# Output product 4 by a second level of Strassen, spread over four slots

## The chip, the cores and the metric

The kernel runs on one core of one Trainium2 chip. The metric is the device time of one launch in microseconds (us), the median of several runs. A profile of one launch stands beside it: start, duration and names of every instruction on the five engines, which are the matrix engine (PE in the profile; its weight loads are PEld), the vector engine (DVE), the scalar engine (ACT), GpSimd (POOL) and SyncE (SP), which here only issues transfers.

## What is computed

The reference is a linear attention, followed by two dense layers with a leaky ReLU between them, all in float32:

```python
kv  = einsum('bhsd,bhse->bhde', k, v)          # 8 batches, 8 heads, 576 rows, 64 wide
out = einsum('bhsd,bhde->bhse', q, kv)
x   = out / sqrt(mean(out*out, -1) + 1e-6) * g_norm   # then (4608, 512)
h   = x @ w_in                                 # 512 -> 2048
y   = maximum(0.01*h, h) @ w_out               # 2048 -> 512
```

## The kernel before

The 4608 rows are cut into nine blocks of 512. Block 0 is multiplied plainly. For blocks 1 to 8 each of the two layers is done in four chunks of the hidden width (`NC` = 4), and each chunk of a layer is one Strassen multiplication in Winograd's form: seven products in place of eight, numbered 1 to 7, whose factors (the "sides") are blocks of the matrices or sums of such blocks. Chunk `n` counts through all blocks: block `i` has n = 4(i-1) to 4(i-1)+3, so blocks 3 to 8 begin at n = 8. I write c for n modulo 4.

In blocks 2 to 8 the first layer has a second level: each of the seven products is itself done as seven products of quarter size (`product_h_two`). One *slot* is one outer product of the first layer: seven matmuls of 128 x 128 x 128, in two PSUM banks (`h_ha` and `h_hb`, in the next slot `h_hc` and `h_hd`, and so on in turn), followed by whatever is placed beside it. A chunk has seven slots, called t = 0 to 6 here, with the outer products in the order 1, 2, 6, 5, 7, 3, 4.

The second layer (`product_o`) runs late: the products of chunk n begin at t = 2 of chunk n+1 and end at t = 1 of chunk n+2, one in each slot after the slot's part of the first layer. Its order in blocks 2 to 8 is `(1, 5, 6, None, 7, 3, 4)`; at `None` the slot has no product of the second layer. Products 1, 6, 7 and 4 are summed one after another in one PSUM bank (`o_a` in even chunks, `o_c` in odd ones), products 5 and 3 in the other; after each product the vector engine adds the bank to one of four output tiles in SBUF (the scalar engine copies it where c = 0 and the tile is new). So product 4 finds 1+6+7 in its bank and the tile of rows 2, columns 1 ("21") takes the whole sum. A bank is written again only after it has been read.

Product 2 of the second layer is already done by a second level (class `Second`): its seven quarter products are matmuls of 128 columns into the free fourth column group of the banks `h_hb` and `h_hd`, one in each slot of chunk n+2, read by the vector engine (`o<-h_hb`, `o<-h_hd`, 128 x 128). Its sums of activation quarters, `gi`, are made on GpSimd by `inner_g`, at t = 4 and 6 of chunk n+1; the sums of weight quarters are made once by `inner_w2`.

Within a slot the instructions of the vector engine stand in program order (they are pinned): first the reads of the slot's first-layer banks, then pieces of the next batch's attention and the sums of the next block's x (around the start of chunk c = 3 these are four sums of 128 x 512 more, two of them at t = 0 and 1), then the read of the second layer's bank. The fresh banks of the first layer are copied by the scalar engine; its order is the scheduler's. At the end of a chunk, after product 4 of the first layer, seven additions on the vector engine (`g<-...`) form the hidden activations and four leaky ReLUs on the scalar engine follow, before the scalar engine's second copy of the next chunk's first slot.

The weight sides of the second layer that are sums (products 5, 6 in `t12`; 7, 4 in `t34`) are kept in DRAM and loaded by SyncE for each chunk: `t12` after product 6, `t34` after product 4 of the chunk before.

Of the kernel before, what the change touches and what calls it, by code (L numbers as in the profile page):

```python
# [23 lines left out]
def kernel(  # L24
# [74 lines left out]
    NW = U * NE * P  # L99
    w1_all = consts.tile([P, 2 * NC * NW], F32, name="w1_all")  # L100
    stage = consts.tile([P, 3 * NW], F32, name="stage")
    pairs = consts.tile([P, 4 * NW], F32, name="pairs")
    g_all = [consts.tile([P, 4 * U * N2], F32, name=f"g_{i}") for i in range(2)]

    def view(t, lo, *shape):
        n = 1
        for d in shape:
            n *= d
        t = t[:, lo:lo + n]
        names = "abcd"[:len(shape)]  # L110
        return t.rearrange(f"p ({' '.join(names)}) -> p {' '.join(names)}",
                           **dict(zip(names, shape))) if len(shape) > 1 else t

    def pair(i, *shape):
        return view(pairs, i * NW, *shape)

    def matmul(*args, **kw):
        pin(nc.tensor.matmul(*args, **kw))  # L118
# [66 lines left out]
    zeros = view(g_all[0], 0, NT)  # L185
    nc.vector.memset(zeros[:, :64], 0.0)
    nc.vector.memset(zeros[:, 64:], 0.0)
    ident = consts.tile([P, P], F32, name="ident")

    def make_ident():  # L190
        pin(nc.gpsimd.memset(ident, 1.0))
# [449 lines left out]
    def sides_w1(c):  # L641
# [9 lines left out]
        def more():  # L651
# [5 lines left out]

    w2_dram = [[dram.tile([P, 2, U, N2], F32, name=f"w2_{c}_{i}") for i in range(2)]
               for c in range(NC)]
    t12, t34 = pair(2, 2, U, N2), pair(3, 2, U, N2)  # L660
    writes = []

    def sides_w2(n):

        c = n % NC
        b11, b12 = w2_sb[0][c][:, :, :N2], w2_sb[0][c][:, :, N2:]
        b21, b22 = w2_sb[1][c][:, :, :N2], w2_sb[1][c][:, :, N2:]

        def sums(i):
            t = (t12, t34)[i]
            if n >= NC:
                pin(nc.sync.dma_start(t, w2_dram[c][i]))
                return
            if i == 0:
                add(nc.gpsimd, t[:, 0], b12, b11, True)
                add(nc.gpsimd, t[:, 1], b22, t[:, 0], True)
            else:
                add(nc.gpsimd, t[:, 0], b22, b12, True)  # L680
                add(nc.gpsimd, t[:, 1], b21, t12[:, 1], True)
            if (n, i) == (NC - 1, 1):

                writes.append((w2_dram[c][i], t))
            else:
                pin(nc.sync.dma_start(w2_dram[c][i], t))
        return {1: b11, 2: b21, 3: b22, 5: t12[:, 0], 6: t12[:, 1], 7: t34[:, 0],
                4: t34[:, 1]}, sums
# [49 lines left out]
    def read(to):  # L738
        nonlocal n_read
        while n_read < min(to, len(reads)):  # L740
# [5 lines left out]
    qc = pair(0, 4, 3, P)  # L746
    xt1 = [work.tile([P, 2, N2], F32, tag="xt1", name="xt1"),
           view(w1_all, RING * NG + 24 * P, 2, N2)]
    xt24 = [work.tile([P, 2, 2, N2], F32, tag="xt24", name="xt24"),
            view(w1_all, RING * NG + 16 * P, 2, 2, N2)]  # L750
    xi = view(stage, 0, 3, 7, P)

    def sides_x(i):


        x = xTs.pop(i)
        b11, b12 = x[:, :2, :N2], x[:, :2, N2:]
        b21, b22 = x[:, 2:, :N2], x[:, 2:, N2:]
        home = i % 2 if i > 1 else 0
        t1, t2, t4 = xt1[home], xt24[home][:, 0], xt24[home][:, 1]  # L760
        if i == 1:
            t4 = opool.tile([P, 2, N2], F32, tag="o", name="xt4", bufs=6)
        t3 = b12
        sides = {1: b11, 2: b21, 3: b22, 4: t4, 5: t1, 6: t2, 7: t3}

        def sums():
            for t, a, b in ((t1, b12, b11), (t2, b22, t1), (t3, b22, b12), (t4, b21, t2)):
                add(nc.vector, t, a, b, True)
                yield

        batches, quarters, at = [], {k: {} for k in ORDER}, 0
        upper, lower = (x[:, h:h + 2, :].rearrange("p r (t v n) -> p t r v n", t=2, v=2)
                        for h in (0, 2))
        for js, y in (((1, 7), upper), ((2, 3), lower),
                      ((6, 4), xt24[home].rearrange("p t r (v n) -> p t r v n", v=2)),
                      ((5,), t1.rearrange("p r (v n) -> p r v n", v=2).unsqueeze(1))):
            terms = [y[:, :, r, v, :] for r in range(2) for v in range(2)]
            terms += [xi[:, k, at:at + len(js), :] for k in range(3)]
            batches.append(terms)
            for n, j in enumerate(js):  # L780
                for k, term in zip((1, 7, 2, 3, 5, 6, 4), terms):
                    quarters[k][j] = term[:, n, :]
            at += len(js)

        def inner(kind):
            for y11, y12, y21, y22, t1, t2, t4 in batches:
                if kind == 0:
                    add(nc.gpsimd, t1, y12, y11, True)
                    add(nc.gpsimd, t2, y22, t1, True)
                elif kind == 1:  # L790
                    add(nc.gpsimd, y12, y22, y12, True)
                else:
                    add(nc.gpsimd, t4, y21, t2, True)

        return sides, quarters, sums(), inner
# [83 lines left out]

    gi = view(pairs, 12 * P, 4, P)

    def inner_w2(c):
        y = w2_sb[1][c]
# [7 lines left out]

    def inner_g(c, half):

        g = g_of(c)[3]
        a11, a21, a12, a22 = (g[:, n, :] for n in range(4))
        s1, s2, s3, s4 = (gi[:, n, :] for n in range(4))
        if half == 0:
            add(nc.gpsimd, s1, a21, a22)  # L900
            add(nc.gpsimd, s2, s1, a11, True)
        else:
            add(nc.gpsimd, s3, a11, a21, True)
            add(nc.gpsimd, s4, a12, s2, True)

    class Second:
# [17 lines left out]
        def done(self, k, bank):  # L924
            v, s = INTO[k]
            to = self.o[:, v, s * P:s * P + P]
            add(nc.vector, to, bank, to)
            if self.n % NC == NC - 1 and k == ORDER[-1]:
                self.finish("11", self.o)

    def product_h_two(i, c, quarters, to, second):

# [41 lines left out]
    def product_o(n, g_sides, os, finish, second):  # L974

        c = n % NC
        w_sides, _ = sides_w2(n)
        sums = sides_w2(n + 1)[1] if n + 1 < NC * (NB - 1) else lambda i: None
        if c == 0:

            for key in ("12", "22", "11", "21"):
                os[key] = opool.tile([P, 2, N2], F32, tag="o", name=f"o{key}", bufs=6)


        pieces = ((0, slice(0, N2)), (1, slice(0, P)), (1, slice(P, N2))) \
            if n + 1 == NC * (NB - 1) else None
        into = {1: ("11", True), 5: ("22", True), 2: ("11", False), 6: ("12", True),
                3: ("12", False), 7: ("22", False), 4: ("21", True)}

        def done(i, bank):  # L990
            key, fresh = into[i]
            if isinstance(bank, list):
                for at, (end, (part, cols)) in enumerate(zip(bank, pieces)):
                    to = os[key][:, part, cols]
                    add(nc.vector, to, end, to)
                    if i == ORDER[-1]:
                        finish(key, os[key], part, cols, (nc.sync, nc.scalar)[at % 2])
                if i == 7:
                    finish(key, os[key])
                return  # L1000
            to = os[key].rearrange("p u (v n) -> p (u v) n", v=2)
            if c == 0 and fresh:
                nc.scalar.copy(to, bank)
            else:
                add(nc.vector, to, bank, to)
            if c == NC - 1 and i in (2, 7, 3, 4):
                finish(key, os[key])

            if i == (6 if second else 5):
                sums(0)  # L1010
            elif i == 4:
                sums(1)


        yield from strassen((("oa", "oc"), ("oc", "oa"))[n % 2], lambda i, part, r: g_sides[i][:, 2 * r + part, :],
                            lambda i, part, r: w_sides[i][:, r, :], done,
                           (1, 5, 6, None, 7, 3, 4) if second else ORDER,
                           pieces=pieces)

    def go(steps, n=None):  # L1020
        while n is None or n > 0:
# [16 lines left out]
    def first_block(between):  # L1038
# [26 lines left out]
                       start=(now[2] == 0), stop=(n == 2 * NC * U))  # L1065
            between(n, 1)
        for t in range(4):
            o = opool.tile([P, DM], F32, tag="o", name="o", bufs=6)
            if t % 2:
                nc.scalar.copy(o, accs[t])  # L1070
            else:
                nc.vector.tensor_copy(o, accs[t])
            nc.scalar.dma_start(out[t * P:(t + 1) * P, :], o)
# [45 lines left out]
    HELD = (22, 24, 26)  # L1119
    o_queue, waited = collections.deque(), 0  # L1120

    seconds = {}

    def second_of(n):
        if n in seconds:
# [9 lines left out]
    for i in range(1, NB):  # L1135
# [4 lines left out]
        for c in range(NC):  # L1140
# [3 lines left out]
            for t in range(7):  # L1144
# [22 lines left out]
                if now - 1 in seconds:  # L1167
                    for half in range(2):
                        if t == (6 if half else 4):
                            inner_g((now - 1) % NC, half)  # L1170
                    if t == 5 and now <= 2 * NC:
                        inner_w2((now - 1) % NC)
                if slot == 4 and not one:
                    while writes:
                        pin(nc.sync.dma_start(*writes.pop()))
# [78 lines left out]
```

## Time and profile before

| | before |
|---|---|
| time, median of 3 | 918.09 us (917.85 to 918.37) |
| span of the profiled launch | 916.1 us, TensorE clock granted 1.000 |
| PE busy | 909.3 us, 99% |
| weight loads | 776.3 us, 85% |
| DVE busy | 631.6 us, 69% |
| ACT busy | 328.2 us, 36% |
| POOL busy | 370.2 us, 40% |
| DMA | 200.05 MB, mean 218 GB/s |

The page gives the busy time of each engine, the span in 40 slices, the chain of work that ended last, and the costliest groups of instructions; single stretches are read from the timeline, one line for each run of like instructions (start, duration, engine, names, shapes, and in brackets the idle time before it with what ended it). A float32 matmul of the program stands in the trace as two records, so a product of four matmuls shows as x8. Durations of PE records overlap; what a matmul takes is read from the distance between starts. The blocks of the second-level part begin, by the first bank `h_ha` of each, at 228.4 (block 2), 326.9, 423.8, 520.7, 617.6, 712.1 and 803.9 us (block 8); the next batch's attention has no more pieces in block 8, and few in block 7.

### The profile page before, as it was taken

To read this page: it belongs to the slowest core of one execution; us is meant where nothing else is said; L and a number is where in the kernel's file an instruction comes from. 1 tells how busy PE (TensorE), PEld (TensorE's weight loads), DVE (VectorE), ACT (ScalarE), POOL (GpSimd) and SP (SyncE) were. 2 spreads that over 40 slices of the span, in tenths; PEclk is the share of its full clock that TensorE was granted. 3 is DMA by queue.
4 is the path that set the end of the run, shared out by engine and by line. 5 is a ranking of instruction groups with operands and counts; after the bars stand their busy time and mean duration, and the time that the engine had idled before them with its cause. 6 is when DMAs were issued, how large, how long until landed. Compare 5 with 4: busy or idle time off the path is not lost.

```text
span 916.1 us, 18037 instructions
## 1 busy us (share of the span) xinstructions
PE 909.3 (99%) x6980; PEld 776.3 (85%) x6980; DVE 631.6 (69%) x1168; ACT 328.2 (36%) x645; POOL 370.2 (40%) x438
## 2 busy tenths in 40 slices
PE   9999999999999999999999999999999999999998
PEld 5444448888998999899999999999999999999997
DVE  4876995587457876587756786678659755755565
ACT  5454533242135233533343324332343333223330
POOL 2000355967633473226421642264226422642222
DMA  8999926885599778776886789658765676667632
GB/s 269 236 245 249 248 85 191 280 285 167 166 360 289 228 209 268 233 230 214 255 247 230 219 249 272 222 178 212 242 183 176 187 222 198 185 185 223 197 109 92
DMA packets 90228, 200.05 MB, mean 218 GB/s; under 512 B 9888, under 2 KB 42272, under 8 KB 90144
## 3 DMA queue, kind: packets, MB, share of 16 engines
q1 hardware_dynamic: 79680, 187.04, 68.6%
q10 hardware_dynamic: 10016, 10.69, 3.4%
q8 instruction: 55, 0.90, 0.4%
q0 software_dynamic: 448, 1.18, 0.3%
q14 instruction: 29, 0.24, 0.1%
HBM read 172.39 MB, written 26.48 MB: 217 GB/s over the span
## 4 chain that ended last, share of the span: by engine, by line
PE 96%; DMA 2%; DVE 1%; issue 0%; ACT 0%; POOL 0%; SPq 0%; ACTq 0%; DVEq 0%; POOLq 0%
PE o_a L118 19%; PE o_c L118 18%; PE h_ha L118 11%; PE h_hb L118 11%; PE h_hc L118 8%; PE h_hd L118 8%; PE o_acc L118 6%; PE h_ps L118 6%; PE o_ps L118 3%; PE h_a L118 2%; PE h_b L118 1%; PE h_c L118 1%; PE h_d L118 1%; PE kv_ps L118 1%; DMA pairs<-in_v_dram 1%; DMA v_in<-in_v_dram 1%
## 5 line engine op out<-in xcount | busy, mean ns | idle before, releaser
L637 POOL TENSOR_TENSOR gs<-g 128x512 f32<-128x512 f32 x64 | 81.7, 1277 | 253.3 <-ACT g L833 253.3
L833 ACT ACTIVATE g<-g 128x512 f32<-128x512 f32 x124 | 78.2, 631 | 131.9 <-DVE g L637 131.9
L952 ACT COPY w_all<-h_ha 128x512 f32<-128x512 f32 x84 | 48.9, 582 | 173.5 <-PE h_ha L118 167.8
L118 PE MATMUL o_a<-pairs,gs 128*128 128x256 f32 x384 | 91.3, 381 | 0.0
L118 PE MATMUL o_c<-pairs,gs 128*128 128x256 f32 x376 | 89.2, 380 | 0.0
L637 DVE TENSOR_TENSOR o<-h_hb,o 128x128 f32<-128x128 f32 x104 | 29.8, 287 | 83.8 <-ACT pairs L952 83.7
L637 DVE TENSOR_TENSOR o<-o_c,o 128x512 f32<-128x512 f32 (+1 forms) x91 | 61.2, 672 | 23.9 <-PE o_c L118 23.6
L118 PEld LDWEIGHTS o_a<-pairs,gs 128*128 128x128 f32 x384 | 69.8, 190 | 9.2 <-POOL pairs L637 1.2
L118 PEld LDWEIGHTS o_c<-pairs,gs 128*128 128x128 f32 x376 | 68.3, 190 | 7.6
L637 DVE TENSOR_TENSOR o<-o_a,o 128x512 f32<-128x512 f32 x75 | 51.2, 683 | 28.2 <-PE o_a L118 28.1
L637 POOL TENSOR_TENSOR pairs<-w_all 128x512 f32<-128x512 f32 x8 | 11.1, 1384 | 120.6 <-ACT cut L245 102.3
L118 PE MATMUL h_ha<-stage,w_all 128*128 128x128 f32 x448 | 59.6, 276 | 0.0
L118 PEld LDWEIGHTS h_ha<-stage,w_all 128*128 128x128 f32 x448 | 56.6, 192 | 3.0 <-issue 0.7
L118 PE MATMUL h_ps<-xT,w_all 128*128 128x512 f32 (+1 forms) x136 | 58.0, 570 | 0.9 <-DVE w_all L258 0.9
L118 PE MATMUL o_acc<-w,g 128*128 128x512 f32 x128 | 57.8, 595 | 0.0
L637 DVE TENSOR_TENSOR g<-g,pairs 128x512 f32<-128x512 f32 x84 | 55.7, 689 | 1.9
L637 POOL TENSOR_TENSOR pairs<-g 128x128 f32<-128x128 f32 x52 | 23.9, 459 | 75.4 <-PE h_hb L118 46.7
L118 PEld LDWEIGHTS h_ps<-xT,w_all 128*128 128x128 f32 x136 | 25.5, 190 | 30.0 <-issue 26.6
L637 DVE TENSOR_TENSOR w_all<-h_hc,w_all 128x512 f32<-128x512 f32 x56 | 38.3, 684 | 15.9 <-PE h_hc L118 15.8
L118 PEld LDWEIGHTS o_acc<-w,g 128*128 128x128 f32 x128 | 24.0, 190 | 29.8 <-issue 29.4
L637 DVE TENSOR_TENSOR o<-h_hd,o 128x128 f32<-128x128 f32 x78 | 22.1, 283 | 37.8 <-ACT pairs L952 37.7
L118 PE MATMUL h_hb<-stage,w_all 128*128 128x128 f32 x336 | 46.7, 275 | 0.0
(228 smaller groups left out, 2264.6 us busy)
## 6 DMA issues: line engine op xcount, KB each, us to landing
w_all<-w SPq DMA_DIRECT2D x196, 448.0 KB, 4.2
pairs<-w SPq DMA_DIRECT2D x56, 512.0 KB, 4.3
out_dram<-o ACTq DMA_DIRECT2D x35, 256.0 KB, 4.6
v_in<-in_v_dram SPq DMA_DIRECT2D x29, 288.0 KB, 5.7
k_in<-in_k_dram SPq DMA_DIRECT2D x28, 288.0 KB, 5.1
q_in<-in_q_dram SPq DMA_DIRECT2D x56, 144.0 KB, 6.0
q_in<-in_q_dram SPq DMA_DIRECT2D x56, 140.0 KB, 5.8
w<-stage SPq DMA_DIRECT2D x12, 512.0 KB, 4.6
```

The source lines that it names most:

```text
L118: pin(nc.tensor.matmul(*args, **kw))
L637: ins = eng.tensor_tensor(out_, a, b_, op=ALU.subtract if minus else ALU.add)
L833: nc.scalar.activation(t, t if src is None else src, func=AF.Prelu, alpha=SLOPE)
L952: nc.scalar.copy(q[:, at], bank)
```

## The change

For chunks n = 8 to 28 (blocks 3 to 7, and the first chunk of block 8: 21 chunks) product 4 of the second layer is no longer four matmuls of 256 columns but seven of 128 columns, a second level as for product 2. It is for saving matrix work: seven quarter products for eight. The parts:

- `Fourth` does the seven in four steps, `(1, 2, 5), (6, 3), (7,), (4,)`, in a fresh tile of the bank that products 1, 6 and 7 have used, in column groups 0 to 2. Step 0 stands in the slot where product 4 was (t = 1 of chunk n+2); steps 1, 2 and 3 stand at t = 2, 3 and 4, after the next chunk's own product of that slot. Each step's matmuls are followed by the vector engine's adds of 128 x 128 into the tile "21" (copies on the scalar engine for c = 0 and quarters 1, 5, 6, 4).
- The order of the other products becomes `(1, None, 6, 5, 7, 3, None)`: the second step is now the empty one, product 5 moves from t = 3 to t = 5, product 6 stays at t = 4.
- As product 4 no longer finds 1+6+7 in its bank, product 7 is added into a tile of its own ("7"), and for c = 3 (and at n = 28) that tile is added to "22" and to "21" by two more additions of 128 x 512.
- `inner_g` makes the sums of quarters for products 2 and 4 at once (128 x 256 in place of 128 x 128). The weight quarters of product 4 with their sums are made once in block 2 (`inner_w4`), written to DRAM, and loaded (448 KB) in place of the 256 KB of the old side 4.
- Output tiles: "11" has two buffers of its own, the others four; the identity matrix takes the place of a tile that is used later.

```diff
+    def four(n):
+        return 2 * NC <= n < NC * (NB - 1) - 3
...
+    class Fourth:
+        STEPS = (1, 2, 5), (6, 3), (7,), (4,)
+        COLUMN = {1: 0, 6: 0, 7: 0, 4: 0, 2: 1, 5: 2, 3: 2}
...
+        def step(self, at):
+            if at == 0:
+                self.bank = ps_m.tile([P, 4, P], F32, tag=self.tag, name=f"f_{self.tag}")
+            for k in self.STEPS[at]:
+                matmul(self.bank[:, self.COLUMN[k], :], lhsT=self.left[k], rhs=self.right[k],
+                       start=(k == 1), stop=True, skip_group_check=True)
+            for k in self.STEPS[at]:
+                bank = self.bank[:, self.COLUMN[k], :]
+                v, s = INTO[k]
+                to = self.o_of("21")[:, v, s * P:s * P + P]
+                if self.n % NC == 0 and k in (1, 5, 6, 4):
+                    nc.scalar.copy(to, bank)
+                else:
+                    add(nc.vector, to, bank, to)
+            if at == 3:
+                self.last()
...
         def done(i, bank):
             key, fresh = into[i]
+            if fourth and i == 7:
+                key, fresh = "7", True
...
-            if c == NC - 1 and i in (2, 7, 3, 4):
+            if fourth and i == 7:
+                sums(1, 0)
+                if c == NC - 1 or not four(n + 1):
+                    add(nc.vector, os["22"], os["22"], os["7"])
+                if c == NC - 1:
+                    finish("22", os["22"])
+            elif c == NC - 1 and i in (2, 7, 3, 4):
                 finish(key, os[key])
...
+        def last():
+            sums(1, 1)
+            if c == NC - 1 or not four(n + 1):
+                add(nc.vector, os["21"], os["21"], os["7"])
...
+        before = fourths.popleft() if fourths else None
+        order = ORDER
+        if fourth or before:
+            order = (1, None, 6, 5, 7, 3, None if fourth else 4)
+        elif second:
+            order = (1, 5, 6, None, 7, 3, 4)
...
+        for j in range(7):
+            next(steps)
+            if before and j < 3:
+                before.step(j + 1)
+            if fourth and j == 6:
+                now.step(0)
+            yield
...
     def inner_g(c, half):
-        g = g_of(c)[3]
-        a11, a21, a12, a22 = (g[:, n, :] for n in range(4))
-        s1, s2, s3, s4 = (gi[:, n, :] for n in range(4))
+        g = view(g_all[c % 2], 0, 4, 4, P)
+        a11, a21, a12, a22 = (g[:, n, 2:, :] for n in range(4))
+        s1, s2, s3, s4 = (gi_two[:, :, n * P:n * P + P] for n in range(4))
```

## The prediction

> **What bounds the kernel now.** I read the page first: busy times, then the chain that ended last.
>
> ```profile
> PE 909.3 (99%) x6980; PEld 776.3 (85%) x6980; DVE 631.6 (69%) x1168; ACT 328.2 (36%) x645; POOL 370.2 (40%) x438
> ...
> PE 96%; DMA 2%; DVE 1%; issue 0%; ACT 0%; POOL 0%; SPq 0%; ACTq 0%; DVEq 0%; POOLq 0%
> ```
>
> The matrix engine never rests, so matrix work that goes away is time that goes away, as long as no wait takes its place. Next I read the price of a matmul and the spare time of the other engines, in the timeline of one chunk start (block 3, c = 3, which begins at 398.83), PE first:
>
> ```profile
> 404.12 1.89 PE L118 MATMUL o_c<-pairs,g 128*128 128x256 f32 x8
> 405.85 1.05 PE L118 MATMUL h_ha<-stage,w_all 128*128 128x128 f32 x8
> 406.75 0.83 PE L118 MATMUL h_hb<-stage,w_all 128*128 128x128 f32 x6
> ...
> 407.73 0.77 PE L118 MATMUL o_ps<-qT,kv 64*32 64x320 f32 x16
> 408.43 1.28 PE L118 MATMUL o_ps<-v_in,k_in 64*64 64x64 f32 x72
> 409.64 1.99 PE L118 MATMUL o_a<-w,g 128*128 128x256 f32 x8
> 411.47 0.72 PE L118 MATMUL h_hc<-stage,w_all 128*128 128x128 f32 x5
> ```
>
> The first line is product 4 at t = 1: 1.73 us to the next start for four matmuls of 256 columns, 0.4325 us each. The second: 0.89 us for four of 128 columns, 0.2225 each. So the first layer's eight matmuls of a slot take 1.78 us, a full slot 3.51 us. Now the vector engine in the same stretch:
>
> ```profile
> 401.19 1.48 DVE L637 TENSOR_TENSOR g<-g,w_all 128x512 f32<-128x512 f32 x2
> 402.70 2.02 DVE L637 TENSOR_TENSOR g<-g,pairs 128x512 f32<-128x512 f32 x3
> 405.78 0.29 DVE L637 TENSOR_TENSOR o<-h_hb,o 128x128 f32<-128x128 f32 x1 [1.06 <-ACT pairs L952]
> 405.99 1.28 DVE L637 TENSOR_TENSOR xT<-xT 128x512 f32<-128x512 f32 x1
> 407.20 0.68 DVE L637 TENSOR_TENSOR o<-o_a,o 128x512 f32<-128x512 f32 x1
> ...
> 410.14 0.68 DVE L637 TENSOR_TENSOR o<-o_c,o 128x512 f32<-128x512 f32 x1
> ...
> 411.65 0.90 DVE L372 TENSOR_TENSOR sum<-sum,sq 128x320 f32<-128x320 f32 x2 [0.38 <-ACT sq L368]
> 412.46 0.69 DVE L637 TENSOR_TENSOR o<-o_a,o 128x512 f32<-128x512 f32 x1
> ```
>
> What to see: the bank `h_hb`, filled at t = 0, is read at 405.78 to 406.07, and the matrix engine writes it again at 406.75: 0.68 us to spare. Product 4, done at 405.85, is read only at 410.14, and product 1, done at 411.37, at 412.46. At 69% on the average the vector engine is behind here, working off the g additions that follow every chunk. Last, what happens when such a read is late (block 7, c = 3; PE, then DVE):
>
> ```profile
> 789.24 0.39 PE L118 MATMUL h_hb<-w,pairs 128*128 128x128 f32 x2
> 789.76 1.99 PE L118 MATMUL o_a<-w,g 128*128 128x256 f32 x8
> 791.60 1.05 PE L118 MATMUL h_hc<-stage,w_all 128*128 128x128 f32 x8
> ```
>
> ```profile
> 789.03 0.68 DVE L637 TENSOR_TENSOR o<-o_a,o 128x512 f32<-128x512 f32 x1
> ```
>
> `o_a` could start at 789.46 but starts at 789.76, 0.05 us after the read ends (789.71), and takes 1.84 in place of 1.73: 0.05 of latency and 0.11 of restart for each wait. The table of waits misses this: it lists a pause of the weight loads only.
>
> **What the Trainium skill says.** "PSUM — Partial Sum Buffer", section "PSUM bank collisions raise a hardware error": no two of matrix, scalar and vector engine may touch one bank at a time, not even two readers, nor different columns; the program has to keep them apart. The trace agrees: "DVE o L637 <- ACT pairs L952: 121.5, 91, 3.2" heads the vector engine's waits; `o<-h_hb` starts 0.03 us after the scalar engine's copy out of the same bank's other columns. So I take a step of `Fourth` to wait for all reads of the step before, not only for its own column's. "VectorE: DVE Perf Modes", section on the errata, prices a float32 tensor_tensor at (N+151)/0.96 ns: 691 and 291 for 512 and 128 columns; here 684 and 287, but in a row they start 0.60 and 0.20 apart, and I count with those. "SBUF — State Buffer", section "SBUF: two separate sides": the port pair that the vector engine and GpSimd share is locked for an instruction with two SBUF inputs. The trace agrees: `xT<-xT` takes 1.28 us above, beside a GpSimd addition, and 0.68 alone.
>
> **The change, part by part.**
>
> *Matrix work.* 4 x 0.4325 = 1.73 goes, 7 x 0.2225 = 1.56 comes: 0.17 us for each of 21 chunks, 3.6 us in all. This is the whole of the gain.
>
> *Where it goes from.* Slot t = 1 loses 1.73 - 0.67 = 1.06, t = 2 gains 0.445, t = 3 loses 1.51, t = 4 gains 0.22, t = 5 gains 1.73. So from t = 2 to t = 4 the matrix engine comes to the banks 0.6 to 2.1 us earlier than now, while the vector engine's backlog is what it was: the three quarter adds of step 0 start 0.20 apart and cost just the 0.60 of product 4's add. That is a subtraction that this trace shows once: in the last chunk t = 1 has no second-layer product, and the spare time at `h_hb` is 878.71 - 878.44 = 0.27, where full slots have 2.0 (a difference of 1.73).
>
> *First wait: `h_hb` at t = 2.* The spare times by chunk c = 0, 1, 2, 3 are 1.4, 2.0, 1.0 to 2.0, and 0.67, less 1.06. For c = 1 the new add "22" += "7" stands among the g additions, minus 0.60 more: 0.3 left. For c = 2 product 7 goes to the scalar engine, 0.6 more. For c = 3 it is -0.4: a wait. Who stands behind it: all of the matrix engine.
>
> *Second wait: step 1 at t = 2* needs step 0 read. Ready (from the chunk's first matmul) = start of product 4's read now + 0.40 + 0.28 + 0.05. Wanted: 3.51 + 2.45 + 3.51 plus attention in the slot.
>
> *Third wait: step 2 at t = 3*, with only 1.78 us of first layer since step 1. Ready = start of product 1's read now + 0.60 + 0.20 + 0.28 + 0.05; wanted 2.22 after step 1. The reads now, wanted and ready for each chunk start (the later steps' loss holds the earlier's, as they wait on one backlog):
>
> | chunk start | step 1 wanted, ready | step 2 wanted, ready | loss |
> |---|---|---|---|
> | c=3, 398.83 | 11.59, 12.04 | 13.81, 14.76 | 0.95 |
> | c=3, 495.61 | 11.69, 12.04 | 13.92, 14.94 | 1.02 |
> | c=3, 592.40 | 11.80, 12.03 | 14.03, 15.12 | 1.09 |
> | c=3, 687.97 | 10.70, 12.04 | 12.93, 15.26 | 2.33 |
> | c=3, 780.65 | 9.89, 12.02 | 12.12, 13.40 | 2.13 |
> | c=0, 423.80 | 9.48, 10.11 | 11.70, 12.37 | 0.67 |
> | c=0, 520.69 | 9.48, 9.94 | 11.70, 12.21 | 0.51 |
> | c=0, 617.58 | 9.48, 10.05 | 11.70, 12.32 | 0.62 |
>
> In blocks 6 and 7 the attention beside t = 2 of c = 3 is shorter, so steps 1 and 2 come earlier; hence the large losses. For c = 0 two transposes of q (1.25 us each) are in the backlog; blocks 7 and 8 have none and lose nothing. Other c = 1 and c = 2 starts have 0.3 us or more left, but 373.86 loses 0.17. Sum 9.3 + 0.2, and 0.11 of restart for nine chunks: 10.5 us.
>
> *The rest at nothing.* Step 3 and product 5 behind it have 3.5 and 1.78 us, with the vector engine caught up by t = 4 (product 6 is read within 0.2 to 0.9 us there). Product 7's own tile costs the same add as before. `inner_g` grows on GpSimd by some 0.3 us an instruction (0.46 for 128 columns, 0.73 for 256), hidden by three slots until step 0. The weights' 192 KB more for each chunk are asked for four slots ahead (14 us; such loads land in 4.3). The scheme in block 2 (four GpSimd additions, one write) has three slots; SyncE stands behind the write, but the first layer's ring is five slots deep.
>
> Net: 10.5 - 3.6 = +6.9: **925.0 us**.
>
> **The rivals.** *All hidden, 914.5 us:* 918.1 - 3.6. For it: PE at 99% and DVE at 69%; the scheduler could order the scalar engine's copy of `h_hb` before the leaky ReLUs. Against it: that mends the first wait alone. Chance 0.15. *Waits by column, 922.9:* a step waits for its own column's read: 0.40 and 0.20 less, loss 8.4 in all. Against it stands the wait between engines that read different columns. Chance 0.10. *Only the two large ones stay, 919.2:* the small losses are differences of some 0.5 to 1 us that a better order of attention pieces could swallow; 4.5 + 0.2 - 3.6 = +1.1. Chance 0.10. *More waits, 929:* for c = 2 starts the reads of a step alternate between scalar and vector engine in one bank, each waiting for the other; six times 0.5 us, and five times 0.2 at c = 1: +4 on top. Chance 0.15.
>
> **How the numbers follow.** The main case has 0.50, so 925.0. Leaving out the hidden case (0.15) and the end of the last (0.04), the range is 917 to 929.5. Faster 0.15, same 0.09 (most of the third rival, 919.2 lies within 0.2% of 918.1), slower the other 0.76.
>
> **What would show it.** Right: pauses of the matrix engine of 0.5 to 2 us at t = 2 and 3 of chunks c = 3 and c = 0, ended by the vector engine's reads of `o`; fewer PE records' time by 3.6 us, a longer span; DVE busy up a little. Wrong: starts of 2.0 us between t = 3 and t = 4 with no pause after c = 3 starts; or pauses that end on a DMA, on GpSimd or on the scalar engine.

## The result, and the profile after

The changed kernel takes 929.52 us (median of 4 runs, 928.00 to 930.19) against 917.97 (917.57 to 918.37) for the kernel before in the same session: ratio 1.0123 (95% interval 1.0106 to 1.0141), 11.5 us slower. The forecast was 925.0, so the sign held and the loss came out 4.6 us larger; 929.5 was the upper end of the range. The profiled launch spans 927.6 us against 916.1, both at a granted clock of 1.000.

The page of after, the busy line and the chain that ended last:

```profile
PE 911.6 (98%) x7106; PEld 778.1 (84%) x7106; DVE 653.6 (70%) x1282; ACT 333.2 (36%) x669; POOL 407.6 (44%) x454
...
PE 85%; DVE 10%; DMA 3%; ACT 1%; issue 1%; POOL 0%; ACTq 0%; SPq 0%; DVEq 0%; POOLq 0%
```

The busy shares hardly moved (99% to 98%). The chain did: 96% matrix engine has become 85%, and the vector engine, 1% before, holds 10%. Time that was pure matrix work now passes through reads by the vector engine. (PE busy rose by 2.3 us, where the forecast named 3.6 us less as a sign. It counts records, whose modelled ends overlap the next start, so it does not measure the matrix work that was saved; the slots below do.) The waits of the matrix engine in blocks 2 to 8 of after, a table that is empty for the same stretch of before (columns: who waits for whom, us in total, times, longest):

```profile
PE f_oc L118 <- DVE o L638: 3.5, 6, 1.0
PE o_a L118 <- DVE o L638: 2.6, 4, 1.2
PE h_ha L118 <- DMA w_all<-w: 1.2, 1, 1.2
PE h_hb L118 <- DVE o L638: 1.1, 5, 0.2
PE o_c L118 <- DVE o L638: 0.9, 1, 0.9
```

`f_oc` are steps of `Fourth`, `h_hb` the first bank that the forecast named, and most of the `o_a` line is a product whose wait it did not have. The last line is in truth a wait for a load, as shown further down. The table counts a pause from the modelled end of the record before, which lies some 0.17 us after the next could start (0.39 us for a pair of records that start 0.2225 apart), and leaves short pauses out. (The forecast took it to list pauses of weight loads alone; that was a misreading.) So to size the waits I set the start of every slot of after against the same slot of before and took off the shifts that the moved matmuls make by themselves (-1.06, +0.445, -1.51, +0.22, +1.73 us at t = 1 to 5). What is left, in us:

| | b2 | b3 | b4 | b5 | b6 | b7 | sum |
|---|---|---|---|---|---|---|---|
| c=3, t=2 and 3: `h_hb`, steps 1 and 2 | | 1.23 | 1.31 | 1.38 | 1.96 | 2.27 | 8.2 |
| c=0, t=2 and 3: steps 1 and 2 | | | 0.33 | 0.34 | 0.34 | | 1.0 |
| c=1, t=2 | | | | | | 0.12 | 0.1 |
| c=0, t=5: product 5 | | | 0.05 | 0.45 | 0.85 | 1.43 | 2.8 |
| waits for loads | 1.4 | 1.2 | | | | | 2.6 |

With 0.4 us more before block 2 and the matrix work's 3.6 us less, that makes 15.1 - 3.6 = 11.5.

The steps at c = 0 of block 4, first the vector engine of after:

```profile
435.26 1.25 DVE L456 STREAM_TRANSPOSE qT<-q_in 128x576 f32<-128x576 f32 x1
436.35 0.81 DVE L638 TENSOR_TENSOR o<-f_oa,o 128x128 f32<-128x128 f32 x3
437.08 0.28 DVE L638 TENSOR_TENSOR o<-h_hb,o 128x128 f32<-128x128 f32 x1
437.27 1.25 DVE L456 STREAM_TRANSPOSE qT<-q_in 128x576 f32<-128x576 f32 x1
438.37 0.68 DVE L638 TENSOR_TENSOR o<-o_c,o 128x512 f32<-128x512 f32 x1
438.97 0.60 DVE L638 TENSOR_TENSOR o<-f_oa,o 128x128 f32<-128x128 f32 x2
```

and the matrix engine there:

```profile
435.44 1.89 PE L118 MATMUL o_c<-w,g 128*128 128x256 f32 x8
437.21 0.49 PE L118 MATMUL f_oa<-stage,pairs 128*128 128x128 f32 x2
...
439.33 0.39 PE L118 MATMUL h_hd<-w,pairs 128*128 128x128 f32 x2
439.62 0.49 PE L118 MATMUL f_oa<-stage,pairs 128*128 128x128 f32 x2
```

The three reads of step 0 end at 436.35 + 0.81 = 437.16; step 1, which writes columns 0 and 2, starts 0.05 us later. Step 2 starts 0.05 us after the second read of step 1 (438.97 + 0.60 = 439.57), though it writes column 0 and the last read is of column 2. Without a wait the two steps could have begun only 0.04 and 0.07 us earlier, so this alone proves little. At c = 3 of block 4 the same step 2 shows it better:

```profile
513.86 0.61 DVE L638 TENSOR_TENSOR o<-f_oc,o 128x128 f32<-128x128 f32 x2
```

```profile
513.59 0.39 PE L118 MATMUL h_hd<-w,pairs 128*128 128x128 f32 x2
514.52 0.49 PE L118 MATMUL f_oc<-stage,pairs 128*128 128x128 f32 x2 [0.54 <-DVE o L638]
```

It could begin at 513.81. The first of the two reads, that of its own column, is over by about 514.15 (one such read takes 0.29), the second at 514.47; the step begins at 514.52. So a step waits for the whole bank, as the forecast took it, and not by column.

What it missed, at t = 5 of c = 0 in block 7, vector engine and then matrix engine:

```profile
736.92 0.70 DVE L401 STREAM_TRANSPOSE inv<-spread 128x512 f32<-128x512 f32 x1
737.66 1.23 DVE L403 TENSOR_TENSOR xT<-xT,inv 128x1024 f32<-128x1024 f32 x1
738.80 0.68 DVE L638 TENSOR_TENSOR o<-o_c,o 128x512 f32<-128x512 f32 x1
739.40 0.28 DVE L638 TENSOR_TENSOR o<-f_oa,o 128x128 f32<-128x128 f32 x1
```

```profile
738.19 0.39 PE L118 MATMUL h_hd<-w,pairs 128*128 128x128 f32 x2
739.74 1.56 PE L118 MATMUL o_a<-pairs,gs 128*128 128x256 f32 x6 [1.16 <-DVE o L638]
```

Product 5 writes the bank that step 3 has just used. Step 3's read (ending at 739.68) stands behind the last of the attention, 1.9 us of it, and behind product 6's read. Product 5 could begin at 738.41 and begins at 739.74.

### The profile page after: what moved, and what is told of

The parts are those of the page before. It is cut to its first block, busy times and chain, and to the rows that moved or that the text cites. A ratio compares the mean times of both kernels' runs of the same rounds, so it can differ in the third digit from the quotient of the medians.

```text
span 927.6 us, 18532 instructions
## 1 busy us (share of the span) xinstructions
PE 911.6 (98%) x7106; PEld 778.1 (84%) x7106; DVE 653.6 (70%) x1282; ACT 333.2 (36%) x669; POOL 407.6 (44%) x454
## 4 chain that ended last, share of the span: by engine, by line
PE 85%; DVE 10%; DMA 3%; ACT 1%; issue 1%; POOL 0%; ACTq 0%; SPq 0%; DVEq 0%; POOLq 0%
PE o_c L118 14%; PE o_a L118 14%; PE h_ha L118 9%; PE h_hb L118 9%; PE h_hc L118 7%; PE h_hd L118 7%; PE o_acc L118 6%; PE h_ps L118 6%; DVE o L638 2%; DVE g L638 2%; PE o_ps L118 2%; PE f_oa L118 2%; PE h_a L118 2%; PE h_b L118 1%; PE f_oc L118 1%; PE h_c L118 1%
## 5 line engine op out<-in xcount | busy, mean ns | idle before, releaser
L638 DVE TENSOR_TENSOR o<-o_c,o 128x512 f32<-128x512 f32 (+1 forms) x81 | 54.5, 672 | 27.8 <-PE o_c L118 27.4
L638 DVE TENSOR_TENSOR o<-o_a,o 128x512 f32<-128x512 f32 x64 | 43.8, 684 | 25.8 <-PE o_a L118 25.6
L638 POOL TENSOR_TENSOR pairs<-g 128x256 f32<-128x256 f32 x52 | 38.3, 736 | 34.0 <-PE h_hd L118 19.5
L1012 ACT COPY pairs<-h_hb 128x384 f32<-128x384 f32 x84 | 39.9, 475 | 15.4 <-PE h_hb L118 14.7
L118 PE MATMUL h_ha<-xT,w_all 128*128 128x128 f32 x224 | 43.3, 275 | 1.2 <-DMA w_all<-w 1.2
```

The costliest lines, as they stand in the source:

```text
L638: ins = eng.tensor_tensor(out_, a, b_, op=ALU.subtract if minus else ALU.add)
L1012: nc.scalar.copy(q[:, at], bank)
```

## Experiments

Theories, as the expectations name them. **W**: what is lost are waits of the matrix engine for late reads of banks. **D**: the vector engine has too much work, whatever is read when. **P**: the other parts (weights' transfers, the write and sums in block 2, GpSimd) cost the time. In these sessions the kernel before itself ran between 917.3 and 928.1 us, and several profiles lost up to 7.9 us ahead of block 2, at loads of the attention's v and at a lower granted clock after them. So two measures stand side by side: the ratio to before, and, from the trace, the time from the first matmul of block 2 to the start of block 8's last slot, free of that first stretch.

| run | ratio (95% interval) | blocks 2 to 8, us |
|---|---|---|
| before | 1 | 660.0 |
| after | 1.0123 (1.0106 to 1.0141) | 671.2 |
| e1_rest_only | 1.0011 (0.9985 to 1.0038) | 661.1 |
| e2_no_bank_reads | 1.0069 (1.0045 to 1.0092) | 666.2 |
| e3_swap_5_7 | 1.0133 (1.0089 to 1.0176) | 671.6 |
| e4_reads_early | 1.0132 (1.0071 to 1.0192) | 670.6 |
| e5_reads_early_sums_later | 1.0117 (1.0089 to 1.0146) | 669.1 |
| e6_and_write_later | 1.0100 (1.0076 to 1.0123) | 668.2 |
| e7_before_same_order | 0.9995 (0.9978 to 1.0013) | 659.6 |
| e8_quarters_not_added | 1.0019 (1.0002 to 1.0037) | 660.7 |
| e9_reads_early_three | 1.0165 (1.0132 to 1.0199) | 671.9 |
| e10_and_write_on_gpsimd | 1.0063 (1.0038 to 1.0088) | 665.0 |
| e11_sums_behind_reads | 1.0057 (1.0032 to 1.0081) | 665.4 |
| e12_write_on_gpsimd_only | 1.0081 (1.0049 to 1.0113) | 668.9 |

### The other parts alone

```diff
     def four(n):
-        return 2 * NC <= n < NC * (NB - 1) - 3
+        return False
```

> The changed kernel with no chunk done by the second level (the condition for it is never true): product 4 is one product of 256 columns again in the old order, but the wider GpSimd sums, the weight quarters made and written in block 2, the two kinds of output tiles and the moved identity stay. Theory W (the loss is the matrix engine waiting for late reads of the new bank and of the banks that come due earlier): 918.0 + 3.0 = 921.0 us, from 918.4 to 922, since the 1.4 us in block 2, the 1.2 us in block 3 and the 0.4 us in block 1 have nothing to do with the quarters. Theory P (the other parts cost most of it): 926 or more. Theory D (the vector engine's added work is the bound): 918 to 919, as that work is gone.

Ratio 1.0011, no difference to be told. Its slots equal before's except for one wait of 1.15 us at t = 6 of block 3's first chunk. P falls as the main cause; that one wait is its share, and is taken up again below. (This run also loads the old side of 256 KB for every chunk; the larger loads are judged by e8 below.)

### Are the bank's reads the cause?

```diff
             for k in self.STEPS[at]:
-                bank = self.bank[:, self.COLUMN[k], :]
                 v, s = INTO[k]
+                bank = self.o_of("7")[:, v, s * P:s * P + P]
                 to = self.o_of("21")[:, v, s * P:s * P + P]
```

> The quarter products are made, but the additions after them take quarters of the tile of product 7 in SBUF in place of the bank, so product 4 is left out of the output. The vector engine has as many additions as in the changed kernel, in the same order, but no step has to wait for a read of its bank, nor has product 5. Theory W: 914.5 + 3.0 of the other parts + about 2 us (the wait for h_hb in chunks c = 3 stays) = 919.5 us. Theory D: 929, as the vector engine's work is the same.

Neither: 666.2 us lies halfway, for a reason of its own. Its vector engine at c = 3 of block 4:

```profile
511.25 1.36 DVE L638 TENSOR_TENSOR o<-o,o 128x128 f32<-128x128 f32 x1
```

An add with two inputs in SBUF beside a GpSimd instruction took 1.36 us, the longest of these adds, where the add from the bank takes 0.29 (without GpSimd beside it such an add took as little as 0.26); the adds that were to stay the same did not. This is the shared port that the prediction cites from the Trainium skill ("SBUF — State Buffer", section "SBUF: two separate sides"), and I should have thought of it before the run. The trace agrees: GpSimd's addition there ends at 512.46, this add at 512.61. The run decides nothing. A cleaner one leaves the seven adds out:

```diff
             for k in self.STEPS[at]:
-                bank = self.bank[:, self.COLUMN[k], :]
-                v, s = INTO[k]
-                to = self.o_of("21")[:, v, s * P:s * P + P]
-                if self.n % NC == 0 and k in (1, 5, 6, 4):
-                    nc.scalar.copy(to, bank)
-                else:
-                    add(nc.vector, to, bank, to)
+                if self.n % NC == 0 and k == 4:
+                    nc.scalar.copy(self.o_of("21"), self.o_of("7"))
```

> The changed kernel without the additions and copies after the quarter products: product 4 is left out of the output. The vector engine has 126 additions less, and the bank of the quarters is never read. In the run that kept the additions with sources in SBUF they disturbed, as they shared the port with GpSimd. Theory W: the waits of the steps and of product 5 go, those for h_hb in c = 3 (0.43 each) and what else comes due 1.06 us earlier stay: 914.4 + 3.0 + 2.2 = 919.6 us, with 2 to 3 us of waits in blocks 3 to 7.

Ratio 1.0019, 660.7 us. The waits of its matrix engine in blocks 2 to 8 are down to these:

```profile
PE o_c L118 <- DVE o L638: 1.0, 1, 1.0
PE h_hb L118 <- DVE o L638: 0.8, 5, 0.2
PE o_a L118 <- DVE o L638: 0.7, 1, 0.7
```

No step waits, nor product 5 after step 3, and the loads of 448 KB are all still there, so they are not the cause. What stays is `h_hb` at c = 3 (0.43 us in each of blocks 3 to 6, 0.93 with its product in block 7: 2.65) and 1.26 in block 3, at the load. That these reads are the cause is shown. Whether a read is late by its place in the queue or by the amount of work ahead of it is not: the run takes both away.

### Moving the reads forward

The next runs keep all work and change only what stands ahead of the reads. First, products 5 and 7 change places (the additions of product 7's tile go behind product 5):

```diff
...
-            order = (1, None, 6, 5, 7, 3, None if fourth else 4)
+            order = (1, None, 6, 7, 5, 3, None if fourth else 4)
```

> Products 5 and 7 of the second layer change places (7 at t = 5, 5 at t = 6), with the additions of the tile of product 7 after product 5. Product 5 needs the bank that the quarters have used, and now comes one slot later. Theory W: the waits at t = 5 of chunks c = 0 go (0.05, 0.45, 0.85 and 1.43 us in blocks 4 to 7, with their restarts), 929.5 - 2.8 = 926.7 us, nothing else moves. Theories P and D: 929.5.

A miss: 671.6. The waits at t = 5 of c = 0 shrank only to 0.28, 0.68 and 1.25 in blocks 5 to 7. Each c = 3 got a new one of 0.88 at t = 0, where product 3 waits for product 5's read, and lost as much less at t = 2 and 3: 8.2 us at c = 3 in all, as in after. One wait for another. Besides, product 7, now a slot earlier, waited 2.3 us for its load in block 3's second chunk. Then the second layer's product and step are placed ahead of the attention's pieces of their slot:

```diff
+    EARLY = (1, 2, 3, 4)
...
+                    early = i > 2 and t in EARLY and not (slot in HELD and i == NB - 1)
+                    if early:
+                        go_o()
...
-                if slot in HELD and i == NB - 1:
+                if slot in HELD and i == NB - 1 or not one and early:
```

> In slots t = 1 to 4 of blocks 3 to 8 the second layer's products, the quarter steps and their reads stand ahead of the attention pieces and of the sums of x; no work is added or left out, only the order in each engine's queue changes. Theory W: the quarters are read before 1.15 to 1.25 us of other work, and where attention has matmuls in the slot these now stand between step 1 and step 2. The waits at steps 1 and 2 and at t = 5 go, that for h_hb at c = 3 stays (5 times about 0.45 us): 929.5 - 7.3 - 2.8 = 919.4 us. Theory D: 929, the vector engine's work is the same. Theory P: 929.

Half a hit. With the same work, all waits at c = 0, those of the steps and of product 5 (3.8 us), are gone: there it was the place in the queue. At c = 3 the slot t = 2 loses 1.54 to 1.55 us in blocks 3 to 6. In block 4 it is 0.4 at `h_hb`; 0.8 at product 1, which now comes before the attention's matmuls and waits for product 3's read behind an x sum; and 0.25 at step 1, which waits for step 0's reads. And the loss at t = 6 of block 3's first chunk, where product 7 waits for its load, grew from 1.2 to 4.8 us with 0.5 in the next slot, which eats the gain. The next run has the reads ahead at t = 0 too, and the sums of the next block's x one slot later (shown against after; the other lines are those of e4):

```diff
+    EARLY = (0, 1, 2, 3, 4)
...
-                        if slot in (20, 21, 22):
-                            go(sums, 2 if slot == 20 else 1)
+                        if slot in (21, 22, 23):
+                            go(sums, 2 if slot == 21 else 1)
```

> As the run with early reads, now also at t = 0, and the four sums of the next block's x moved from the slots t = 6, 0, 1 around the start of c = 3 to t = 0, 1, 2, behind the reads. No work is added or left out. Theory W': what is left of the waits in c = 3 (1.5 us at t = 2, for the read of product 3, and 0.45 us for h_hb) stands behind those sums in the vector engine's queue; it goes, and of the 12 us of waits in blocks 3 to 7 less than 1.5 us stay in the trace. The time: 918.0 - 3.6 + 1.8 of blocks 1 and 2 + 1 + the stall at t = 6 of c = 0 in block 3, which is 1.2 to 5.4 us: 918.4 to 922.6. Theory D (vector engine's work): 929.

669.1: c = 3 still loses 1.30 us in each of blocks 3 to 6, now at step 1, behind the x sums. The same two moves in the kernel before:

> The kernel before the change with the same two moves in the queues (second layer's products and reads ahead of attention at t = 0 to 4, sums of x later). It has one pause of the matrix engine of 0.4 us in blocks 3 to 8 to win: 917.6 us. If the order of the queues were good for something else than the waits, it would gain as much as the changed kernel does, 10 us or more.

0.9995, 659.6 us: the moves took its one pause of 0.4 us and no more. They are worth nothing to a kernel that has no waits.

### The wait for weights

In block 2 SyncE writes product 4's quarters to DRAM and must wait for GpSimd's four sums. SyncE in after, at the first chunk of block 3:

```profile
339.10 1.73 SPq L159 DMA_DIRECT2D q_in<-in_q_dram  x4
345.27 0.34 SPq L1088 DMA_DIRECT2D w<-pairs  x1
345.66 0.54 SPq L1089 DMA_DIRECT2D w<-stage  x1
346.30 0.39 SPq L761 DMA_DIRECT2D w_all<-w  x1
346.73 0.46 SPq L683 DMA_DIRECT2D pairs<-w  x1
```

From 340.8 to 345.3 it issues nothing. The last line loads the side of product 7, lands 4.1 us later, and the product, whose bank had been read at 347.19, starts at 350.97. The first try, on top of e5, has SyncE load that half first and write later:

```diff
-                later.extend(([1, lambda: (
+                later.extend(([1, lambda: sums(1, 0)], [4, lambda: (
...
-                    [2, lambda: sums(1)]))
+                    [5, lambda: sums(1, 1)]))
```

> As the run before, and the write of product 4's weight quarters in block 2 and the start of block 3 is put three slots later in SyncE's queue, with the load of product 7's side before it. Theory W' with SyncE's queue as cause of the stall in block 3: that stall goes too, and the time is 914.4 + 0.4 of block 1 + 1.4 or less of block 2 + 1 = 915 to 917.2 us, less than the kernel before. If the stall is from the traffic and not from the queue, 918 to 922.

668.2: the wait at t = 6 went, and a loss of 4.0 us came at t = 1 and 2 of the next chunk. There SyncE asks for the other half, the side of product 4, only at 355.56, when the write asked for at 348.81 has ended; it lands 3.5 us later, and product 4 starts at 359.21 in place of 356.93, 2.3 us late. The other 1.7 us are the matrix engine's clock, as in e4, e5 and e9. From e9, over product 7 of the same place:

```profile
353.00 0.39 PE L118 MATMUL h_hb<-w,g 128*128 128x128 f32 x2
358.22 3.75 PE L118 MATMUL o_c<-pairs,gs 128*128 128x256 f32 x8 [4.83 <-DMA pairs<-w]
361.76 0.63 PE L118 MATMUL h_ha<-xT,w_all 128*128 128x128 f32 x2
```

```profile
359.00:361.00 2.00, 2.00 (x6) 0.50 1.03 409
```

(In the last line the clock stands behind the busy time.) Product 7 waits 5.0 us, from 353.22 to 358.22, and then its four matmuls take 3.54 us in place of 1.73, at a clock of 0.50. So e9 loses 7.1 us here, 2.1 of them to the clock. In e4, e5 and e6 the pauses are 3.6, 3.7 and 2.3 us, and the clock adds 1.7 each. The pauses of 1.1 us in after and 2.3 us in e3 have no low clock behind them; no run tests what decides it.

The second try takes the write off SyncE, alone in the last run of all (the half for product 7 is again asked for ahead of it):

```diff
-                later.extend(([1, lambda: (
-                    pin(nc.sync.dma_start(w4_dram[c][:, :4, :], f4)),
-                    pin(nc.sync.dma_start(w4_dram[c][:, 4:, :], f4_more)))],
-                    [2, lambda: sums(1)]))
+                later.extend(([1, lambda: sums(1, 0)], [2, lambda: (
+                    pin(nc.gpsimd.dma_start(w4_dram[c][:, :4, :], f4)),
+                    pin(nc.gpsimd.dma_start(w4_dram[c][:, 4:, :], f4_more)))],
+                    [4, lambda: sums(1, 1)]))
```

> The kernel after with nothing moved but the write of product 4's weight quarters in block 2: asked for by GpSimd in place of SyncE, the loads into the two halves of that side one and four slots after. If SyncE's standing behind that write is what was missing in the forecast's costs at nothing: the waits of 1.42 us in block 2 (c = 1, t = 3 and 4) and of 1.2 us at t = 6 of block 3's first chunk go, a span of 925 in place of 927.6, ratio about 1.0095. If the transfers are too many in themselves, both waits stay and the span is 927 to 928.

SyncE at the same place:

```profile
345.70 1.72 SPq L159 DMA_DIRECT2D q_in<-in_q_dram  x4
347.46 0.42 SPq L683 DMA_DIRECT2D pairs<-w  x1
347.98 3.03 SPq L761 DMA_DIRECT2D w_all<-w  x2
```

No gap, and no wait at t = 6. From 671.2 to 668.9: 0.9 us in block 3, 1.4 in block 2. The first is shown to be SyncE standing behind the write. The second is not: the wait in block 2 (the first layer's `w_all`, 1.35 us) is also missing in the profiles of e1, e3, e4, e5, e8 and e9, whose block 2 is that of after, so it need not come with the change: a transfer that was late in one launch, as far as these profiles tell.

### Both together

The order is changed once more: c = 3 keeps its old one, and all four x sums stand at t = 2 and 3 of c = 3 (the first pair of lines is against e4, the rest against after).

```diff
-                    early = i > 2 and t in EARLY and not (slot in HELD and i == NB - 1)
+                    early = i > 2 and c < NC - 1 and t in EARLY and not (slot in HELD and i == NB - 1)
...
-                        if slot in (20, 21, 22):
-                            go(sums, 2 if slot == 20 else 1)
-                        if slot == 24:
+                        if slot in (23, 24):
+                            go(sums, 2)
+                        if slot == 25:
                             inner(0)
-                        elif slot == 25:
+                        elif slot == 26:
                             inner(1)
```

> The kernel after, with two moves in the queues: in chunks c = 0, 1, 2 the second layer's product and step stand ahead of the attention's pieces at t = 1 to 4 (c = 3 keeps its order, so that the attention's matmuls still stand between product 1 and the steps), and the four sums of x leave t = 6 of c = 2 and t = 0 and 1 of c = 3 for t = 2 and 3 of c = 3, two at each; the GpSimd additions of x quarters follow one slot later. W (all that stays of the loss is which instructions of the vector engine stand ahead of the reads): the five waits of c = 3 (1.2 to 2.3 us each) fall below 0.5, those of c = 0 and of product 5 stay away as in the earlier order: 918.1 - 3.6 + about 1.5 + 3.0 of blocks 1 to 3 = 919. D (the vector engine has too much to do, in whatever order): waits of 6 us or more in blocks 4 to 7 again, 925 or more. P (weights' transfers): the wait at t = 6 of block 3's first chunk stays at 1.2 to 4.9 in both cases.

With the write moved to GpSimd as well:

> As the run before, and in block 2 the write of product 4's weight quarters is asked for by GpSimd, which makes them, in place of SyncE; the loads into the two halves of that side follow one and four slots after. W: about 916 to 917.5, faster than the kernel before, if the rest of the loss was SyncE standing behind that write: no wait for weights at t = 6 of block 3's first chunk nor in the next one. D: as the run before, 925 or more. If the transfers themselves are too many and not their order, the waits on DMA in blocks 2 and 3 stay at 1 to 5 us.

The pair differs in the write alone: 671.9 against 665.0. In e9 product 7 at block 3 cost the 7.1 us above, in e10 it costs nothing. e10 is 6.2 us better than after in these blocks, and 5 us short of before, against W's forecast of faster. Its steps no longer wait at t = 2 of c = 3, but at t = 3 and 5 the waits are 1.0 to 1.8 us together in blocks 4 to 6, and c = 0 lost 0.74 to 1.0 there. So, last, the x sums behind the slots' reads and GpSimd back in its place:

```diff
-                        if slot in (23, 24):
-                            go(sums, 2)
-                        if slot == 25:
-                            inner(0)
-                        elif slot == 26:
+                        if slot == 25:
                             inner(1)
...
+                if not one and i + 1 < NB and slot in (23, 24):
+                    go(sums, 2)
+                    if slot == 24:
+                        inner(0)
```

> As the last run (reads ahead in c = 0 to 2, write of the weight quarters on GpSimd), but the four sums of x stand behind the second layer's reads of their slots (t = 2 and 3 of c = 3), and the GpSimd additions of x quarters are back where they were, one slot earlier. The last run's waits were 0.3 to 1.2 at t = 3 and 0.5 at t = 5 of c = 3, and 0.3 to 0.7 twice at c = 0, where GpSimd's additions fell beside the g additions (1.0 to 1.2 us in place of 0.69); 8.6 us more matrix time than 918.1 - 3.6 in blocks 3 to 8. W: the waits of c = 3 and c = 0 fall below 0.3, in all under 3 us: a span of 914 to 917 against 916.1, ratio 0.998 to 1.001. D: the vector engine's time has to be paid somewhere, the waits move to other slots and 5 us or more stay: ratio 1.005 or more.

D's line, not W's: 665.4, and c = 3 loses 1.02, 1.28 and 1.75 in blocks 4 to 6, all at t = 5 now; c = 0 loses 0.8 to 0.9 again. For c = 0 the traces name a reason that no run tests alone. In e11, block 4 (begins at 430.65):

```profile
432.26 1.81 DVE L638 TENSOR_TENSOR g<-g,w_all 128x512 f32<-128x512 f32 x2
434.11 2.43 DVE L638 TENSOR_TENSOR g<-g,pairs 128x512 f32<-128x512 f32 x3
```

```profile
432.30 1.23 POOL L638 TENSOR_TENSOR pairs<-g 128x256 f32<-128x256 f32 x1
433.49 1.17 POOL L638 TENSOR_TENSOR pairs<-g,pairs 128x256 f32<-128x256 f32 x1
```

and in e4, which loses nothing at c = 0 (begins at 430.32; GpSimd idle here until 435.52):

```profile
431.32 1.40 DVE L638 TENSOR_TENSOR g<-g,w_all 128x512 f32<-128x512 f32 x2
432.76 2.02 DVE L638 TENSOR_TENSOR g<-g,pairs 128x512 f32<-128x512 f32 x3
```

GpSimd's additions of x quarters wait for the x sums, which come later now, and its sums of activation quarters stand behind those additions. Beside them the g additions of c = 0 are slower and end 5.9 us after the block's start in place of 4.5, and the reads stand behind them. The vector engine at c = 3 of block 4 in e11:

```profile
521.41 0.57 DVE L383 STREAM_TRANSPOSE turned<-sum 128x384 f32<-128x384 f32 x1
522.01 0.55 DVE L384 TENSOR_REDUCE rms<-turned 128x12 f32<-128x384 f32 x1
522.48 0.68 DVE L638 TENSOR_TENSOR o<-o_a,o 128x512 f32<-128x512 f32 x1
523.08 0.28 DVE L638 TENSOR_TENSOR o<-f_oc,o 128x128 f32<-128x128 f32 x1
```

and its busy time from the chunk's first matmul to t = 3, and from there to product 5 (the columns are us, then busy us and instructions of PE, PEld, DVE, ACT and POOL, the clock, DMA):

```profile
502.83:514.97 12.14, 12.14 (x163) 10.91 (x162) 9.15 (x21) 6.15 (x12) 5.02 (x4) 1.00 0.73 232
514.97:523.42 8.45, 7.70 (x63) 7.30 (x61) 8.11 (x19) 1.38 (x3) 3.49 (x5) 1.00 0.71 235
```

The second line shows 8.11 of 8.45 us: from t = 3 to product 5 of c = 3 the vector engine is full in this order. Before that it is not: 9.15 of 12.14 us. In after, with the sums in their old place, it was busy 13.70 of 15.46 us from the start of c = 3 to step 2. The port that is shared with GpSimd is not what fills it here: the four x sums take 0.68 to 0.69 us each in e11's blocks 3 to 7, where in after two of each four take 1.13 to 1.29. In the orders tried, moving work at c = 3 only moved the wait: in block 4 it is 1.3 us at t = 2 and 3 in after, 1.0 at t = 3 and 5 in e10, 1.0 at t = 5 in e11.

## Why the forecast was right in sign and short in size

- *Matrix work, -3.6 us.* Right. Block 8, which has three chunk starts with quarters and no wait in after, is 0.5 us shorter (84.0 against 84.5), 0.17 each.
- *Waits at steps 1 and 2 and at `h_hb`.* Right in cause (e8) and place, 9.3 us for 10.5. The c = 3 starts came as forecast: 1.23, 1.31, 1.38, 1.96, 2.27 for 1.06, 1.13, 1.20, 2.44, 2.24 with the restart. c = 0 came at 1.0 us in all for 2.1: the g additions stood 0.7 us earlier against their block's start than in before (430.12 - 427.69 = 2.43 for 426.94 - 423.80 = 3.14), while the working had kept the backlog fixed.
- *Bank-wide or by column.* Bank-wide, shown above.
- *"The rest at nothing": the step that failed.* It said that step 3 and product 5 behind it have 3.5 and 1.78 us, "with the vector engine caught up by t = 4". At c = 0 of blocks 5 to 7 it had not caught up: 0.45, 0.85 and 1.43 us, 2.8 us with block 4's 0.05. I had looked at product 6's read only, and not at who writes the bank after step 3. e8 (no such wait without step 3's read) and e4 (none with that read ahead of the attention) show it.
- *The same step, SyncE.* It said that SyncE stands behind the write but the first layer's ring is deep enough. The ring did not run dry there; the side of product 7, queued behind the same write, was late: 1.2 us, taken away by e12. It is 3.6 to 5.0 us when other queues are moved (e4, e5, e9), and a lower clock adds 1.7 to 2.1. Left over are 1.4 us in block 2 and 0.4 before it, which no run ties to the change. Pauses that end on a transfer were among the forecast's signs of being wrong; here they are 2.6 us of 15.1.
- *Luck.* The waits that were forecast came 1.2 us smaller and those that were not add 5.8, so the total misses by 4.6: it is nearer than its parts.
- *Rivals.* Three foresaw less than 925: all hidden, by column, and only the two large ones. None came. The fourth had the size (929) but the wrong place, c = 2 and c = 1, which lost nothing and 0.1 us.

W holds for after as it stands: without the reads blocks 2 to 8 take 10.5 us less, of which 1.4 are block 2's. For a repair the question between W and D is open at c = 3. At c = 0 an order without waits exists (e4). At c = 3 no order tried brought a block's loss under 1 us in blocks 4 to 6; but in e11 the vector engine stood idle for 3.0 us just ahead of the stretch in which it was full, so D is not shown either. The x sums spread over c = 0 to 2, or the reads ahead of the attention at t = 3 and 4 of c = 3 alone, were not tried. No order of the changed kernel that was measured beats the kernel before.

## What to carry to other kernels

Before putting more, smaller matmuls into a shared bank, list for each of them who reads the bank last, what stands ahead of that read in its engine's queue, and who writes the bank next, down to the last write: the largest wait that the forecast missed was at a pair that it didn't list. A saving of 0.17 us a chunk cannot pay for a read that is late by 0.2, and a busy engine share of 70% on average says nothing of the 8 us in which it is 96%. A transfer that must wait for an engine is better asked for by that engine than put at the head of the queue that feeds everybody: here that was worth 0.9 us alone, and 6.9 with the other queues moved. And a pause can cost more than its length: see the clock in e9.

## What the runs showed of the hardware

Steps of one bank that write other columns than those being read start 0.05 us after the last read of the bank, at 437.21, 439.62 and 514.52; whether the program's own waits or the bank would ask for it, no run tells. A 128x128 add with both inputs in SBUF took up to 1.36 us beside GpSimd in e2, 4.7 times the 0.29 of the same add from a bank, and 0.26 at the least. Around pauses of the matrix engine of 2.3 to 5.0 us its granted clock stood at 0.50 in e4, e5, e6 and e9, which cost 1.7 to 2.1 us more each; at one of 2.3 us in e3 it did not. Where two things hold an instruction back, the table of waits can name the wrong one: the wait of 0.95 us before 350.97 stands there as the vector engine's, whose last read had ended 3.8 us earlier, and was a load's.
